# Forgetting attention and a GELU MLP on one core: a new order of the start, w_in in six parts, and the low value tile copied by GpSimd

## The chip, the core and the metric

The kernel runs on one core of one Trainium2 chip. The metric is the time of one launch on the device in microseconds; the runs shown are three, and their median counts. The engines are named as in the profile: PE is TensorE (matmuls; PEld its weight loads), DVE is VectorE, ACT is ScalarE, POOL is GpSimd and SP is SyncE. POOL, SP and ACT can issue DMAs. Each engine executes its instructions in the order in which the program gives them and waits on semaphores.

## The reference

```python
def _attn_ref(q, k, v, f):                 # q, k, v: (8, 8, 576, 64); f: (8, 8, 576)
    scores = (1 / sqrt(64)) * q @ k^T
    log_f = np.log(np.clip(f, 0.0001, 1.0))
    cum = np.cumsum(log_f, axis=-1)
    decay = cum[:, :, :, None] - cum[:, :, None, :]
    scores = np.where(causal, -1e9, scores + decay)
    return softmax(scores) @ v

def _moe_ref(x, w_in, w_out):              # x: (4608, 512), w_in: (512, 2048), w_out: (2048, 512)
    h = x @ w_in
    g = 0.5 * h * (1.0 + np.tanh(c * (h + 0.044715 * h * h * h)))
    return g @ w_out                       # (4608, 512) float32
```

The attention's output, with the heads side by side, is the MLP's input x.

## The kernel before

**Quads.** The 64 pairs of batch and head are taken four at a time: quad i (0 to 15) holds four heads of batch i // 2. For each quad, q and k are loaded by POOL's queue (`LQ.i`, `LK.i`, cast to bf16 on the way) and transposed by DVE (`TQ.i`, `TK.i`, line 197). The row factor of the decay falls out of the softmax, so only exp(-cum) of the key is needed: it is worked out once for all quads into `wT` and `w_bf`, and multiplied into v (`vw` by DVE or `VW` by POOL, line 214). The "low" value tile is a copy of the first 64 rows of the product into partitions 64 to 127 (`CL.i`, `copy_low`, line 219).

**Steps of a quad.** `S.i.r` (or `H.i.r.g` for a pair of heads) computes the scores of round r on PE (line 260) and their exps on ACT (line 268), `M.i.r` masks the diagonal blocks on POOL (line 274), `m.i.r` does it by a product with a triangle on DVE (line 303), `D.i` computes the denominators on PE (line 328; for quads 0 and 1 in two parts, `D.i.part`, line 314) and DVE (lines 347 to 351), `V.i.x` or `V.i.x.part` multiplies with the values on PE (lines 328 and 314), and DVE scales the result into xT (line 359).

**The MLP.** Tokens go through the MLP in nine chunks of 512. Chunk 0 is worked in two halves of 256 tokens: `J.half.g` computes 4 of the 16 feature tiles for one half (16 matmuls, line 481, into a two-bank tile of the pool psS) and one gelu on ACT (line 488). Its second product (`F.0.n`, line 597) and those of the other chunks (`F.c.n`, `f.c.n`, line 527; seven products in place of eight) are spread between the attention steps of later quads. Line 552 adds up and stores results through `o_st`.

**The order** is written by hand. `SETUP` and `FRONT` are tables of words, played from left to right, for quads 0 to 6 and chunks 0 and 1; `TABLES[c]` holds chunk c from 2 on, with `q3` meaning quad 2c + 3. Every engine's queue follows this order, and so do the DMA queues of the engines that issue. `A@B` lets the transfer of A wait for that of B. The words of the start: `LP.t` and `LU.t` load tile t of v of batch 0, `LX.b.half` and `LV.b.half` the heads of half of batch b; `SB` is POOL's sums over earlier tiles of the logs, `CW` the two matmuls that complete the log sums and the two exps that give `wT`, `W` the cast to `w_bf`; `TR` makes the triangles and `Z` writes zeros; `WI.c` and `WO.c` load the parts of w_in and w_out on POOL's queue; `B.n.cols` issues n matmuls on zeros into a tile that nobody reads (line 239); `X` and `Y` load ACT's table for exp and for gelu.

**Memory on chip.** The pools in PSUM are psS with two tiles of two banks (scores, MLP block, some outputs), psO with one tile of two banks (`po`, and the tile of the filler matmuls) and psM with two tiles of one bank. A tile comes free when its last reader is done.

Of the kernel before, what the change touches and what calls it, by code (L numbers as in the profile page):

```python
# [16 lines left out]
def kernel(  # L17
# [200 lines left out]
    def copy_low(i):  # L218
        nc.vector.tensor_copy(vw[i % 2][64:128, LOW], vw[i % 2][0:64, 0])
# [202 lines left out]
    def seven_in(c, k, act=0):  # L422
# [47 lines left out]
        gelu(1, 0, u2)  # L470
        yield

    def mlp_in_half(half, g):

        ph = psS.tile([128, 2, 512], FP32, name="ps_h", tag="s")
        n0 = QA * half
        for dts in (range(N_DT - 1), range(N_DT - 1, N_DT)):
            for j in range(4):
                ft = 4 * g + j
                for dt in dts:  # L480
                    nc.tensor.matmul(  # L481
                        ph[:, j // 2, QA * (j % 2):QA * (j % 2) + QA],
                        w_in_sb[:, dt, 128 * ft:128 * ft + 128],
                        xT[:, dt, n0:n0 + QA],
                        start=(dt == 0 and j % 2 == 0), stop=(dt == N_DT - 1),
                        skip_group_check=True,
                    )
# [119 lines left out]
    def setup():  # L607
        nc.sync.dma_start(out=f_sb, in_=f.rearrange("b h s -> (b h) s"))
        dmas["LK.0"] = load_one(k, k_c, 0)
        dmas["LQ.0"] = load_one(q, q_c, 0)  # L610
# [13 lines left out]
        nc.vector.tensor_scalar(f_sb, f_sb, 1e-4, 1.0, op0=ALU.max, op1=ALU.min)  # L624
# [10 lines left out]
    def zeros():  # L635
        for t_ in v_nat:
            nc.gpsimd.memset(t_[64:128, HIGH, :, :], 0.0)
        for t_ in vw:
            nc.gpsimd.memset(t_[0:64, LOW, :, :], 0.0)
        nc.gpsimd.memset(w_bf[0:64, :, LOW, :], 0.0)  # L640
# [41 lines left out]
    def load_values(b, half):  # L682
# [121 lines left out]
```

## Time and profile before

| | us |
|---|---|
| median of three runs (326.24 to 327.14) | 326.45 |
| the profiled execution | 326.83 |
| its span in the profile | 325.1 |
| PE busy | 312.4 |
| DVE busy | 255.9 |
| ACT busy | 206.8 |
| POOL busy | 107.3 |

The profile is one execution. Its times count from the start of the span. A row of its timeline gives start, duration, engine, line, operation, output and inputs, shapes, and how many instructions it merges; in brackets stands how long the engine was idle before and who ended that. Matmuls are pipelined, and the durations of two rows can overlap by some 0.06 us. The granted clock of PE was 0.999 in the mean.

### The profile page before, as it was taken

What the parts mean: (1) busy time and instruction counts of PE and PEld (TensorE: products, weight loads), DVE (VectorE), ACT (ScalarE), POOL (GpSimd) and SP (SyncE); (2) the same over time, 40 slices, a digit from 0 to 9 for tenths busy, and PEclk for the clock granted to TensorE, in tenths of its full rate; (3) what the DMA queues carried; (4) which work ended last, traced back from release to release, by engine and by line L of the source; (5) the groups of instructions that cost most, each with busy time, mean ns of one, the idle gap of its engine ahead of it and who ended that gap; (6) DMA issues with size and microseconds to landing.
All of it is one profiled execution on the core that took longest, in us unless ns stands there. A gap on an engine that the chain in (4) does not pass through costs nothing.

```text
span 325.1 us, 12342 instructions
## 1 busy us (share of the span) xinstructions
PE 312.4 (96%) x5527; PEld 219.0 (67%) x5547; DVE 255.9 (79%) x407; ACT 206.8 (64%) x259; POOL 107.3 (33%) x150
## 2 busy tenths in 40 slices
PE   3999999999999999899999999999999999999995
PEld 1357844544867567576777677667766788788784
DVE  5576138896779899968996899789977979896882
ACT  4685676775857686477857785678666843732830
POOL 8986563440320218410563047302720150000000
PEclk9999999999999999999999999999999999999999
DMA  7999999879102931393119711891120012003013
GB/s 134 202 210 214 181 228 190 163 154 228 49 4 86 176 58 36 67 241 86 36 49 175 172 36 37 150 209 37 34 69 0 4 36 100 2 32 100 0 34 97
DMA packets 46485, 33.45 MB, mean 103 GB/s; under 512 B 29792, under 2 KB 40160, under 8 KB 46432
## 3 DMA queue, kind: packets, MB, share of 16 engines
q0 software_dynamic: 8624, 15.99, 28.3%
q1 hardware_dynamic: 37664, 16.60, 19.4%
q8 instruction: 43, 0.70, 0.9%
q14 instruction: 10, 0.08, 0.1%
q10 hardware_dynamic: 144, 0.07, 0.1%
HBM read 36.85 MB, written 9.44 MB: 142 GB/s over the span
## 4 chain that ended last, share of the span: by engine, by line
PE 87%; DVE 7%; POOL 2%; issue 2%; ACT 1%; POOLq 0%; DVEq 0%; ACTq 0%
PE ps_w L527 27%; PE ps_h L373 14%; PE ps_s L260 9%; PE po L328 9%; PE ps_cd L432 8%; PE ps_ab L432 6%; PE ps_h L481 4%; PE pso L597 4%; PE ps_h L387 2%; PE po_m L314 1%; PE idle_ps L239 1%; DVE pt L303 1%; ACT pt L268 1%; POOL v_nat L168 1%; DVE kT L197 1%
## 5 line engine op out<-in xcount | busy, mean ns | idle before, releaser
L268 ACT ACTIVATE pt<-ps_s 128x1024 bf16<-128x1024 f32 (+2 forms) x100 | 93.7, 988 | 38.5 <-PE ps_s L260 33.1
L274 POOL TENSOR_SCALAR_AFFINE_SELECT pt<-pt 128x512 bf16<-128x512 bf16 (+3 forms) x65 | 38.7, 604 | 115.2 <-ACT pt L268 114.2
L373 PE MATMUL ps_h<-xT,w_in_sb 128*128 128x512 bf16 x228 | 54.5, 379 | 0.6
L527 PEld LDWEIGHTS <-gT 128*32 128x32 bf16 (+1 forms) x1247 | 50.6, 97 | 6.0 <-issue 1.7
L527 PE MATMUL ps_w<-w_out_sb,gT 128*32 128x256 bf16 (+1 forms) x1050 | 46.9, 273 | 0.0
L380 ACT ACTIVATE gT<-ps_h 128x1024 bf16<-128x1024 f32 x30 | 30.6, 1020 | 17.2 <-PE ps_h L373 16.7
L527 PEld LDWEIGHTS <-gsum 128*32 128x32 bf16 (+1 forms) x1256 | 39.2, 97 | 2.5 <-issue 1.1
L373 PEld LDWEIGHTS <-w_in_sb 128*128 128x128 bf16 x240 | 23.4, 98 | 24.3 <-issue 0.4
L260 PE MATMUL ps_s<-qT,kT 32*128 32x64 bf16 (+5 forms) x896 | 36.4, 264 | 0.1
L197 DVE STREAM_TRANSPOSE kT<-k_c 128x576 f32<-128x576 f32 x16 | 19.9, 1245 | 14.1 <-DMA k_c<-in_k_dram 14.1
L527 PE MATMUL ps_w<-usum,gsum 128*32 128x256 bf16 (+1 forms) x832 | 30.6, 273 | 0.0
L214 POOL TENSOR_TENSOR vw<-v_nat,wT 128x1280 bf16<-128x1280 f32 (+1 forms) x13 | 30.3, 2333 | 0.1
L260 PEld LDWEIGHTS <-kT 32*128 32x128 bf16 x896 | 16.5, 93 | 17.1 <-issue 12.0
L441 ACT ACTIVATE gT<-snap 128x512 bf16<-128x512 f32 x45 | 26.1, 625 | 3.0 <-DVE snap L455 2.4
L432 PEld LDWEIGHTS <-w_in_sb 128*128 128x128 bf16 x240 | 23.4, 98 | 6.2 <-issue 1.5
L552 DVE TENSOR_TENSOR o_st<-ps_w,snap 128x512 f32<-128x512 f32 x31 | 21.3, 687 | 7.5 <-PE ps_w L527 6.1
L328 PE MATMUL po<-pt,vw 128*32 128x64 bf16 (+4 forms) x624 | 22.5, 278 | 0.7 <-DVE xT L359 0.7
L359 DVE TENSOR_TENSOR xT<-po,rb 128x576 bf16<-128x576 f32 x26 | 19.5, 751 | 3.8 <-PE po L328 3.3
L328 PEld LDWEIGHTS <-vw 128*32 128x32 bf16 x672 | 14.3, 97 | 11.3 <-issue 4.6
L432 PEld LDWEIGHTS <-xT 128*128 128x128 bf16 x180 | 17.6, 98 | 5.2
L197 DVE STREAM_TRANSPOSE qT<-q_c 128x576 f32<-128x576 f32 x16 | 19.9, 1245 | 0.9 <-PE ps_s L260 0.7
L191 POOL DMA_DIRECT2D k_c<-in_k_dram x16 | 9.2, 576 | 27.8 <-DVE kT L197 22.4
(104 smaller groups left out, 478.1 us busy)
## 6 DMA issues: line engine op xcount, KB each, us to landing
out_dram<-o_st SPq DMA_DIRECT2D x35, 256.0 KB, 2.2
k_c<-in_k_dram POOLq DMA_DIRECT2D x16, 288.0 KB, 5.5
q_c<-in_q_dram POOLq DMA_DIRECT2D x16, 288.0 KB, 7.2
v_nat<-in_v_dram SPq DMA_DIRECT2D x16, 256.0 KB, 6.1
v_nat<-in_v_dram SPq DMA_DIRECT2D x20, 128.0 KB, 4.7
w_in_sb<-in_moe_w_in_dram POOLq DMA_DIRECT2D x4, 512.0 KB, 10.0
w_out_sb<-in_moe_w_out_dram POOLq DMA_DIRECT2D x4, 512.0 KB, 8.6
v_nat<-in_v_dram POOLq DMA_DIRECT2D x9, 128.0 KB, 7.1
```

What stands on the lines that cost most here:

```text
L197: nc.vector.transpose(out=dst.rearrange("p s c -> p (s c)").bitcast(FP32) .rearrange("p (t a) -> p a t", a=S // 32), in_=src.rearrange("p ...
L214: eng.tensor_mul(vw[i % 2][:, t0:t1], vb[:, t0:t1, h0:h0 + 4, :], wT[:, i, t0:t1, :].unsqueeze(3).to_broadcast([128, t1 - t0, 4, D]))
L260: nc.tensor.matmul(tiles[h // 2][:, h % 2, c0:c0 + nq], key_columns(i, key, h, c), qq[32 * h:32 * h + 32, q0:q0 + nq, c], start=(c == 0 an ...
L268: nc.scalar.activation(p[:, 2 * g:2 * g + 2, off:off + n], t[:, :, 0:n], AF.Exp, scale=scale)
L274: nc.gpsimd.affine_select(out=x, in_=x, compare_op=ALU.is_ge, fill=0.0, base=0, pattern=pattern, channel_multiplier=-1)
L328: nc.tensor.matmul(po[r0:r0 + w.shape[-1], 448 + q0:448 + q0 + nq], w, p[:, h, col:col + nq], start=(key in (0, "low")), stop=(key in ("lo ...
L373: nc.tensor.matmul(ph[:, j, :], w_in_sb[:, dt, 128 * ft:128 * ft + 128], xT[:, dt, CH * c:CH * (c + 1)], start=(dt == 0), stop=(dt == N_DT ...
L380: nc.scalar.activation(gT[:, 2 * pr:2 * pr + 2, :], ph, AF.Gelu_apprx_tanh)
L432: nc.tensor.matmul(ps[:, j], w[:, dt, 128 * j:128 * j + 128], x[:, dt], start=(first and j == 0 and dt == 0), stop=(dt == 1), skip_group_c ...
L441: nc.scalar.activation(gT[:, ft:ft + 2, HC * j:HC * (j + 1)], x, AF.Gelu_apprx_tanh)
L527: nc.tensor.matmul(ps[c0:c0 + width, n, cols[0]:cols[1]], x[:, j, 128 * n + c0:128 * n + c0 + width], w[:, j, cols[0]:cols[1]], start=(fir ...
L552: nc.vector.tensor_add(st, ps, kept[name])
```

## The change

- `SETUP` and `FRONT` are written anew up to quad 2. The first matmul of the log sums becomes a word of its own (`CU`); the first scores `S.0.0` stand between it and `CW`, which keeps the second matmul and the exps.
- w_in comes in six parts in place of four: the columns 0 to 512, 512 to 1024 and 1024 to 2048, each in two halves of the rows.
- `mlp_in_half` yields after each of its four feature tiles, and takes its tile from psO where it is called with `spare`. The word `j.0.0` plays one such quarter; four of them stand between the last scores of quads 0 and 1, where fillers stood, and a fifth plays the gelu. `J` plays all. The loop order within it is one feature tile after the other.
- The masks of round 3 of quad 0 go from DVE to POOL (`m.0.3` to `M.0.3`), the second half of v of batch 1 (`LX.1.1`) and quad 3's product (`VW.3`) from the start to behind quad 2's scores.
- The zeros that POOL wrote (`Z`) are written by DVE in `setup`.
- `cl` is `copy_low` on POOL. The tables of chunks 2 to 6 use it in place of `CL` for q3 and q4; it stands behind the masks of q3's last round, and behind `VW` of q4.
- `seven_in` gets a branch for `act` over 1.

```diff
     SETUP = """
-        TK.0 LP.4 LP.0 LP.1
+        TK.0 LP.0 LP.1
     """
     FRONT = """
-        TQ.0 B.2.256 TK.1 SB TR LP.2@LQ.0 B.2.128 CW S.0.0 B.5.384 B.1.256 Z TQ.1 vw.0.0 S.0.2 WI.0 LQ.2 M.0.0 B.3.384 H.1.0.1 LP.3 B.1.256 vw.1.0
-        WI.1@LU.4 W H.1.1.1 WI.3 B.2.256 WI.2 H.1.0.0 M.1.0.1 D.0.0 M.1.0.0 H.0.1.1 V.0.0.0 H.0.1.0 B.2.256 M.0.1 H.1.1.0 V.0.1.0 D.1.0 H.0.3.0
-        B.2.128 V.1.0.0 LX.1.1 H.0.3.1 V.1.1.0 m.0.3.2 H.1.3.0 m.0.3.4 B.1.256 VW.1.1 H.1.3.1 B.4.128 vw.0.1 D.0.1 M.1.3 S.1.2 M.1.1 LK.2 V.0.1.1
-        V.0.0.1 WO.0 J.0.1 D.1.1 J.0.0 WO.1@LV.1.1 V.1.1.1 V.1.0.1 J.0.3 WO.2@WI.1 VW.3 J.1.0 WO.3 LK.3 LQ.3 J.1.1 TQ.2 J.1.3 LQ.4 LX.1.0@WO.2 TK.2
-        J.0.2 J.1.2 X LK.4 F.0.6 TK.3 B.3.256 S.2.0 LK.5 F.0.9 S.2.2 F.0.10 S.2.1 TQ.3 TQ.4 F.0.10 LV.2.0@LK.5 m.2.1 vw.2 TK.4 S.3.0 f.0.1 M.2.2
-        CL.2 LQ.5 M.2.0 D.2 f.0.6 S.3.1 m.3.0 F.0.6 V.2.0 S.3.2 TK.5 LK.6 M.3.2 f.0.7 V.2.1 CL.3 S.4.1 m.3.1 LQ.6 F.0.6 TQ.5 H.4.2.1 D.3 H.4.0.1
+        TQ.0 B.2.256 TR TK.1 SB B.2.128 CU S.0.0 CW B.5.384 B.1.256 TQ.1 W WI.0 WI.1 vw.0.0 LP.2@LQ.0 M.0.0 LP.4 S.0.2 B.3.384 H.1.0.1 H.1.0.0
+        vw.1.0 LP.3 WI.2@LU.1 M.1.0.1 D.0.0 M.1.0.0 WI.3 WI.4 WI.5 H.1.1.1 V.0.0.0 H.0.1.1 V.0.1.0 D.1.0 H.0.1.0 V.1.0.0 M.0.1 LQ.2 LK.2 H.1.1.0
+        M.1.1 V.1.1.0 H.0.3.0 j.0.0 H.0.3.1 j.0.0 M.0.3 H.1.3.0 j.0.0 vw.0.1 H.1.3.1 j.0.0 M.1.3 VW.1.1 H.1.2.0 D.0.1 H.1.2.1 j.0.0 J.0.1 V.0.1.1
+        V.0.0.1 D.1.1 J.0.2 WO.0 WO.1@LU.4 V.1.1.1 V.1.0.1 J.0.3 J.1.0 WO.2@WI.5 WO.3 J.1.1 TQ.2 LK.3 LQ.3 J.1.2 J.1.3 LX.1.0@WO.0 LQ.4 TK.2 X F.0.6
+        LK.4 TK.3 S.2.0 M.2.0 LK.5 F.0.9 S.2.2 M.2.2 LX.1.1@WO.2 F.0.10 S.2.1 TQ.3 TQ.4 F.0.10 LV.2.0@LK.5 m.2.1 vw.2 TK.4 S.3.0 f.0.1 CL.2 LQ.5
+        VW.3 D.2 f.0.6 S.3.1 m.3.0 F.0.6 V.2.0 S.3.2 TK.5 LK.6 M.3.2 f.0.7 V.2.1 CL.3 S.4.1 m.3.1 LQ.6 F.0.6 TQ.5 H.4.2.1 D.3 H.4.0.1 LQ.7 VW.4
...
     TABLES[3] = """
...
-        f.22 S.q3.1 V.q2.0 TK.q4 TQ.q4 M.q3.1 VW.q3 f.18 S.q3.2 V.q2.1 M.q3.2 TK.q5 CL.q3 f.16 S.q4.0 VW.q4 D.q3 M.q4.0 f.18 S.q4.1 TQ.q5 V.q3.0
-        M.q4.1 f.13 V.q3.1 T f.3 CL.q4 S.q4.2
+        f.22 S.q3.1 V.q2.0 TK.q4 TQ.q4 M.q3.1 VW.q3 f.18 S.q3.2 V.q2.1 M.q3.2 cl.q3 TK.q5 f.16 S.q4.0 VW.q4 cl.q4 D.q3 M.q4.0 f.18 S.q4.1 TQ.q5
+        V.q3.0 M.q4.1 f.13 V.q3.1 T f.3 S.q4.2
...
     def load_w_in(c):
-        n, u = D_FF // 2, c % 2
-        s = slice(n * (c // 2), n * (c // 2 + 1))
+        u = c % 2
+        s = slice(*((0, 512), (512, 1024), (1024, 2048))[c // 2])
         return nc.gpsimd.dma_start(out=w_in_sb[:, 2 * u:2 * u + 2, s], in_=w_in_hbm[:, u, :, s])
...
-    def copy_low(i):
-        nc.vector.tensor_copy(vw[i % 2][64:128, LOW], vw[i % 2][0:64, 0])
+    def copy_low(i, eng):
+        eng.tensor_copy(vw[i % 2][64:128, LOW], vw[i % 2][0:64, 0])
...
         multiply(pd, a22, t4, False)
-        nc.vector.tensor_add(u2, pd, u2)
+        if act > 1:
+            z = part()
+            nc.scalar.copy(z, pd)
+            nc.gpsimd.tensor_add(u2, z, u2)
+        else:
+            nc.vector.tensor_add(u2, pd, u2)
...
-    def mlp_in_half(half, g):
-        ph = psS.tile([128, 2, 512], FP32, name="ps_h", tag="s")
+    def mlp_in_half(half, g, spare=0):
+        if spare:
+            ph = psO.tile([128, 1024], FP32, name="ps_h", tag="po").rearrange("p (a n) -> p a n", a=2)
+        else:
+            ph = psS.tile([128, 2, 512], FP32, name="ps_h", tag="s")
         n0 = QA * half
-        for dts in (range(N_DT - 1), range(N_DT - 1, N_DT)):
-            for j in range(4):
-                ft = 4 * g + j
-                for dt in dts:
-                    nc.tensor.matmul(...)
+        for j in range(4):
+            ft = 4 * g + j
+            for dt in range(N_DT):
+                nc.tensor.matmul(...)
+            if j < 3:
+                yield
+        if spare:
+            yield
         nc.scalar.activation(gT[:, 4 * g:4 * g + 4, n0:n0 + QA], ..., AF.Gelu_apprx_tanh)
...
+        for t_ in v_nat:
+            nc.vector.memset(t_[64:128, HIGH, :, :], 0.0)
+        for t_ in vw:
+            nc.vector.memset(t_[0:64, LOW, :, :], 0.0)
+        nc.vector.memset(w_bf[0:64, :, LOW, :], 0.0)
         nc.vector.tensor_scalar(f_sb, f_sb, 1e-4, 1.0, op0=ALU.max, op1=ALU.min)
...
+    def within_tiles():
+        sums.append(psM.tile([128, NT * BH], FP32, name="cum_ps", tag="m"))
+        nc.tensor.matmul(sums[0], utri_f32, logfT, start=True, stop=False)
     def make_w():
-        cum_ps = psM.tile([128, NT * BH], FP32, name="cum_ps", tag="m")
-        nc.tensor.matmul(cum_ps, utri_f32, logfT, start=True, stop=False)
+        cum_ps = sums[0]
         nc.tensor.matmul(cum_ps[:, BH:], ones_f32, before, start=False, stop=True)
...
-        "J": mlp_in_half,
+        "J": lambda half, g: pull(mlp_in_half(half, g), 4),
+        "j": lambda half, g: pull(parts_in.setdefault((half, g), mlp_in_half(half, g, 1)), 1),
```

In the changed kernel the first MLP product of chunk 0 has line 490, its gelu line 501, the second product of chunk 0 line 610.

More of the change, by code (lines that the diff above doesn't have):

```diff
@@ L83 @@
+        H.4.0.0 V.3.1 v.3.0 f.0.3 H.4.2.0 CL.4 I.1.0 m.4.1 U.0 LV.2.1@LQ.5 I.1.4 TQ.6 m.4.2.3 I.1.1 I.1.5 U.1 LV.3.0@LQ.7 LV.3.1 m.4.2.2 TK.6 G.0
+        M.4.0 LK.7 LQ.8 LK.8 I.1.2 I.1.3 U.3 K.1.0 K.1.1 K.1.2 I.1.6 I.1.7 G.1.1.2 U.2 X F.1.16 S.5.0 f.1.26 S.5.1 D.4 M.5.0 f.1.16 S.5.2 V.4.0
+        m.5.2.3 f.1.10 VW.5 V.4.1 K.1.3 CL.5 m.5.2.2 S.6.0 f.1.10 M.5.1 D.5 f.1.7 S.6.1 V.5.1 f.1.12 V.5.0 T.2 S.6.2 vw.6
     """
@@ L469, in seven_in @@
             gelu(0, 1, p1)
+        if act > 1:
+            yield
         gelu(1, 0, u2)
         yield
-    def mlp_in_half(half, g):
-        ph = psS.tile([128, 2, 512], FP32, name="ps_h", tag="s")
-        n0 = QA * half
-        for dts in (range(N_DT - 1), range(N_DT - 1, N_DT)):
-            for j in range(4):
-                ft = 4 * g + j
-                for dt in dts:
[L481 to L487, printed above, removed]
+    def mlp_in_half(half, g, spare=0):
[3 more added lines that the diff above has]
+            ph = psS.tile([128, 2, 512], FP32, name="ps_h", tag="s")
+        n0 = QA * half
+        for j in range(4):
+            ft = 4 * g + j
+            for dt in range(N_DT):
+                nc.tensor.matmul(
+                    ph[:, j // 2, QA * (j % 2):QA * (j % 2) + QA],
+                    w_in_sb[:, dt, 128 * ft:128 * ft + 128],
+                    xT[:, dt, n0:n0 + QA],
+                    start=(dt == 0 and j % 2 == 0), stop=(dt == N_DT - 1),
+                    skip_group_check=True,
+                )
+            if j < 3:
+                yield
+        if spare:
+            yield
         nc.scalar.activation(gT[:, 4 * g:4 * g + 4, n0:n0 + QA],
@@ L633, in setup @@
         nc.scalar.copy(logfT[0:64, HIGH * BH:], ps_lt[0:64, HIGH * BH:])
[L635 to L640, printed above, removed]
     def triangles(copy):
@@ L652, in sums_before @@
                                  logfT[:, t * BH:(t + 1) * BH])
+    sums = []
+    def within_tiles():
+        sums.append(psM.tile([128, NT * BH], FP32, name="cum_ps", tag="m"))
+        nc.tensor.matmul(sums[0], utri_f32, logfT, start=True, stop=False)
     def make_w():
-        cum_ps = psM.tile([128, NT * BH], FP32, name="cum_ps", tag="m")
-        nc.tensor.matmul(cum_ps, utri_f32, logfT, start=True, stop=False)
+        cum_ps = sums[0]
         nc.tensor.matmul(cum_ps[:, BH:], ones_f32, before, start=False, stop=True)
@@ L669, in pull @@
                 return
-    fills = {}
+    fills, parts_in = {}, {}
     dmas = {}
@@ L687 @@
         "w": lambda: cast_w(nc.scalar.copy),
+        "CU": within_tiles,
         "CW": make_w,
@@ L690 @@
         "sb": lambda: sums_before(nc.vector),
-        "Z": zeros,
         "TR": lambda: triangles(nc.vector.tensor_copy),
@@ L702 @@
         "vw": lambda i, *part: make_vw(i, nc.vector, *part),
-        "CL": copy_low,
+        "CL": lambda i: copy_low(i, nc.vector),
+        "cl": lambda i: copy_low(i, nc.gpsimd),
         "TK": transpose_k,
@@ L759 @@
         "LV": lambda c: load_v(c + 2) if c + 2 < B else None,
-        **{name: quads(ops[name]) for name in "S M m D V v VW vw CL TK TQ LK LQ".split()},
+        **{name: quads(ops[name]) for name in "S M m D V v VW vw CL cl TK TQ LK LQ".split()},
     }
```

17 lines of the change are left out of this document (7 added, 10 removed).

## The prediction

> **What bounds the kernel now.** I read the page first (busy times, chain), then the busy times by stretch, then what TensorE (PE) waited for after the start.
>
> ```profile
> PE 312.4 (96%) x5527; PEld 219.0 (67%) x5547; DVE 255.9 (79%) x407; ACT 206.8 (64%) x259; POOL 107.3 (33%) x150
> PE 87%; DVE 7%; POOL 2%; issue 2%; ACT 1%; POOLq 0%; DVEq 0%; ACTq 0%
> 0.00:20.00 20.00, 13.96 (x141) 6.56 (x141) 11.20 (x27) 12.39 (x17) 17.07 (x37) 1.00 0.93 175
> 20.00:40.00 20.00, 19.80 (x291) 15.26 (x290) 10.50 (x20) 12.05 (x15) 14.64 (x18) 1.00 1.13 200
> 40.00:60.00 20.00, 19.63 (x291) 9.66 (x296) 12.78 (x16) 14.83 (x16) 8.10 (x13) 1.00 1.05 210
> 120.00:140.00 20.00, 18.28 (x522) 13.16 (x512) 18.49 (x27) 11.87 (x13) 12.48 (x16) 1.00 0.29 62
> PE ps_w L527 <- DVE o_st L552: 0.9, 1, 0.9
> PE po L328 <- DVE xT L359: 0.7, 1, 0.7
> ```
>
> The stretch rows give busy us of PE, PEld, DVE, ACT, POOL, then granted clock, DMA share and GB/s. PE is the bound nearly everywhere. Time can be won in three ways only: PE work taken away, the thin start, or PE's waits. After 96 us the list of PE's waits holds exactly the two last rows, 0.94 and 0.73 us to two digits (below), both in chunk 2 (120 to 140 us). At the start, part of PE's busy time is filler matmuls, which compute nothing. So this change can win in two places.
>
> **First scores ahead of the log sums.**
>
> ```profile
> 6.82 1.26 DVE L197 STREAM_TRANSPOSE qT<-q_c 128x576 f32<-128x576 f32 x1 [0.21 <-DMA q_c<-in_q_dram]
> 8.76 1.22 PE L657 MATMUL cum_ps<-gsum 128*128 128x256 f32 x2 [1.01 <-POOL gsum L650]
> 9.91 0.83 PE L260 MATMUL ps_s<-qT,kT 32*128 32x256 bf16 x16
> 10.67 1.99 PE L239 MATMUL idle_ps<-usum 128*128 128x384 bf16 x6
> 12.59 0.72 PE L260 MATMUL ps_s<-qT,kT 32*128 32x320 bf16 x8
> 13.94 1.29 DVE L214 TENSOR_TENSOR vw<-v_nat,wT 128x512 bf16<-128x512 f32 x2 [1.64 <-DMA v_nat<-in_v_dram]
> ```
>
> S.0.0 needs qT, ready at 6.82 + 1.26 = 8.08, but stands behind the ones matmul, which waits for GpSimd's sums. Now S.0.0 runs 8.1 to 8.9, the ones matmul 1.22 to 10.15, the same fillers 1.99 to 12.1: S.0.2 starts at 12.1, 0.5 earlier. The weights' exps come later, behind S.0.0's, near 11.2; their first reader, vw.0.0, waits for v until 13.94 anyway, so that costs nothing.
>
> **The first MLP block in quarters.** Between 14 and 24 us scores, exps and fillers alternate.
>
> ```profile
> 14.00:24.00 10.00, 2.33 (x14) 0.76 (x12) 1.00 1.09 200
> 14.79 8.42 ACT L268 ACTIVATE pt<-ps_s 128x768 bf16<-128x768 f32 x10
> 23.58 0.46 PE L260 MATMUL ps_s<-qT,kT 32*128 32x320 bf16 x8
> 24.08 1.30 ACT L268 ACTIVATE pt<-ps_s 128x640 bf16<-128x640 f32 x2 [0.86 <-PE ps_s L260]
> 29.70 1.22 PE L314 MATMUL po_m<-pt,vw 128*32 128x320 bf16 x40
> 30.86 10.65 PE L481 MATMUL ps_h<-xT,w_in_sb 128*128 128x256 bf16 x96
> ```
>
> The first row is for the filler line alone: PE 2.33 us. These fillers go, and j.0.0's 16 matmuls come in: 96 take 10.65, so 16 take 1.78. PE's work up to the last score is then about the same (0.55 less), and 1.78 us leave the run of MLP matmuls behind it, where PE never waits. The exps cannot hide this: 8.42 + 1.30 us of them from about 14.3 end by 24.0, plus small gaps, against 25.4 now. Of the 0.5 gained at the start I keep 0.3, since PE and ACT are now both nearly full up to the last score (which ends at 23.7 in place of 24.04). Front: 1.78 + 0.3 = **2.1 us**. Bounds: 1.3 (the start's gain gone, PE waiting 0.5 more for exps or masks) to 2.8 (0.5 and 0.55 kept in full).
>
> This needs the data in time. Sizes follow from the shapes; the rates are the stretch rows' (3.5 MB by 20 us, 7.5 by 40, 11.7 by 60). Up to the last of the six w_in parts: f 0.15, four k/q 1.18, v of batch 0 1.18, w_in 2.10 = 4.6 MB, so 20 + 1.1/0.200 = 25.5 us. Columns from 1024 on are first read by J.0.2, behind 16 MLP matmuls and 60 po_m ones: 23.7 + 1.78 + 1.83 = 27.3. Up to the last w_out: 7.3 MB, 39 us; the MLP block ends at 30.86 + 10.65 - 2.1 = 39.4. Both fit by a little.
>
> **Other edits of the start.**
>
> ```profile
> 3.65 0.45 DVE L624 TENSOR_SCALAR gsum<-gsum 64x576 f32<-64x576 f32 x1 [1.37 <-DMA gsum<-in_f_dram]
> 9.59 0.98 POOL L637 MEMSET v_nat<- 64x512 f32 x2
> 42.64 0.49 PE L239 MATMUL idle_ps<-usum 128*128 128x256 bf16 x3
> ```
>
> The zeros move to VectorE, ahead of the clamp of f, where 1.37 us are idle; they need about that, so at most 0.2 is lost there. GpSimd loses 0.98 us and more of memsets and gains two issues for w_in, at some 0.73 each (3.63 for five, quoted below). The 0.49 us of fillers before S.2.0 go too: 0 to 0.49; I take 0, since the scores behind them wait for ACT's table change and exps. The branch for act over 1 is never entered: no table gives more than 1.
>
> **The low value tile on GpSimd.**
>
> ```profile
> L219 DVE COPY vw<-vw x14: 220/221/2070, 54.7 to 263.3; 64x256 bf16<-64x256 bf16 x14
> 127.64 2.33 POOL L214 TENSOR_TENSOR vw<-v_nat,wT 128x1280 bf16<-128x1280 f32 x1
> 127.98 2.07 DVE L219 COPY vw<-vw 64x256 bf16<-64x256 bf16 x1
> 130.82 0.62 PE L527 MATMUL ps_w<-w_out_sb,gsum 128*32 128x256 bf16 x16 [0.94 <-DVE o_st L552]
> 134.95 0.87 PE L328 MATMUL po<-pt,vw 128*32 128x512 bf16 x24 [0.73 <-DVE xT L359]
> 134.11 0.63 POOL L274 TENSOR_SCALAR_AFFINE_SELECT pt<-pt 128x512 bf16<-128x512 bf16 x1 [3.05 <-ACT pt L268]
> 7.25 0.26 POOL L648 COPY gsum<-gsum 128x64 f32<-128x64 f32 x1
> ```
>
> Fourteen copies (shortest, median and longest in ns), 0.22 us in the median; the one of 2.07 started inside GpSimd's product and ended with it (130.05 against 129.97). It held up o_st and, through VectorE's queue, xT: PE's two waits. With the copy on GpSimd, o_st can start 2.07 earlier, more than either wait: 0.94 + 0.73 = **1.67 us**, bounds 0.9 to 1.7. GpSimd's own copy is not in the trace: between 0.26 (the small copy) and 2.33 (the product); I take 0.4, nearer the small one. The product for the next quad and its mask stand behind it; 3.05 idle us before GpSimd's next mask cover both copies of the chunk. The other eight that move win nothing, as PE waited nowhere else.
>
> **v and its product moved.** LX.1.1 (five transfers) and VW.3 move from the start to behind M.2.2.
>
> ```profile
> 32.55 2.35 POOL L214 TENSOR_TENSOR vw<-v_nat,wT 128x1280 bf16<-128x1280 f32 x1
> 42.09 3.63 POOL L168 DMA_DIRECT2D v_nat<-in_v_dram  x5 [4.83 <-DMA w_out_sb<-in_moe_w_out_dram]
> 48.60 1.22 POOL L274 TENSOR_SCALAR_AFFINE_SELECT pt<-pt 128x512 bf16<-128x512 bf16 x2 [0.63 <-ACT pt L268]
> 56.78 0.38 DVE L303 TENSOR_TENSOR pt<-pt,causal 128x512 bf16<-128x512 bf16 x1
> 61.08 0.26 DVE L219 COPY vw<-vw 64x256 bf16<-64x256 bf16 x1
> 60.04 1.22 POOL L274 TENSOR_SCALAR_AFFINE_SELECT pt<-pt 128x512 bf16<-128x512 bf16 x2 [4.52 <-ACT pt L268]
> 62.69 0.86 PE L328 MATMUL po<-pt,w_bf 128*32 128x512 bf16 x24
> 67.37 0.59 POOL L191 DMA_DIRECT2D k_c<-in_k_dram  x1
> v_nat<-in_v_dram POOLq DMA_DIRECT2D x9, 128.0 KB, 7.1
> DMA to landing us min/median/max: 5.2/7.1/9.6
> ```
>
> The new gates are early ones: WI.2 waits for LP.1 (landed when vw.0.0 starts, 13.9) with M.1.0 behind it, due near 15.3 with its exps; LX.1.0 waits for the first w_out quarter (5.7 MB, 31 us) instead of the third, with LQ.4, LK.4 and M.2.0 behind it, and M.2.0 isn't due before 40.
>
> In the new time, 2.1 earlier: M.2.2 ends at 47.7, five issues take 3.63, to 51.3. The last v lands at 54.1 by bytes (10.5 MB: 40 + 3.0/0.210) or at 58.4 by the median 7.1 after issue; I take 56. VW.3 ends 2.35 later, 58.4. Behind it on GpSimd stand LK.6 (0.59 at most) and M.3.2 (1.22): 60.2. D.3, which waits for M.3.2, is due at 62.69 - 2.1 = 60.6; CL.3, which waits for VW.3 at the head of VectorE, at 59.0. It just fits: cost 0, up to 2.0 at the late end (58.4 + 2.35 + 0.59 + 1.22 = 62.6 against 60.6).
>
> **Sum.** The profiled execution took 326.83 (span 325.1, 1.7 around it): 326.83 - 2.1 - 1.67 = 323.06. The median of the runs, 326.45, is 0.38 lower: **322.7**. Its own range, from the bounds: 326.45 - 2.8 - 1.7 = 321.9 to 326.45 - 1.3 - 0.9 = 324.2.
>
> **Rivals.**
> A, 0.20: v lands after 56.4, and D.3 waits for M.3.2. For it: 7.1 median. Against it: the backlog is small by then. 0.3 to 2.0 given back: 323.0 to 324.7.
> B, 0.07: VW.3 starts just before the mask product m.3.0 (56.78 - 2.1 = 54.7) and holds it up for as much as 2.35, as the 2.07 copy was. This needs v at 52.4 to 54.7, the early end. Between 0 and 2.35 of it reaches PE; the middle, 1.2, gives 323.9.
> [...]
> [...]
> C, 0.08: the front wins nothing (the quarters wait for w_in or xT, and PE stops later for w_out): 326.45 - 1.67 = 324.8.
> D, 0.09: slower. M.3.2 behind a very late VW.3 again, beyond the whole gain. To lose 3.8 + 1, M.3.2 must end at 65.4, so v land at 61.3, 10 us after the last issue. The longest in the start's v transfers is 9.6, so only with a fuller DMA queue: 327.6 or more.
> E, 0.04: both gains vanish, 326.4.
>
> **How the numbers follow.** The forecast has 0.52. With A, B and C, 0.87 lie between 321.7 and 325.0, which is the range. 0.3% of 326.45, about what a measurement can tell, is 0.98, so faster means under 325.47: 0.52 + 0.20 + 0.07 + 0.08 = 0.87; same 0.04; slower 0.09.
>
> **What would show it.** Right: S.0.0 at 8.1, S.0.2 near 12.1; the last score by 23.7; the MLP block ending at 39.4; no PE wait near 128 to 135; GpSimd's copies at 0.3 to 0.6 us. Wrong: PE waiting at L490 for w_in, at L610 for w_out, or at D.3 (L328) near 60 for GpSimd; VW.3 ending after 58.8; a VectorE L303 of over 1 us near 55; a MLP block that ends after 40.2.

## The result, and the profile after

The changed kernel takes 324.59 us (median of 14 runs, 322.1 to 331.05) against 326.65 (14 runs, 326.22 to 327.14) for the kernel before on the same chip: 2.06 us less, a ratio of 0.993 with an interval of 0.991 to 0.9951. Ratios, here and below, leave out runs more than 1.5% above the fastest of the same kernel: here the three of 330.46, 330.71 and 331.05, whose mean granted clock is 0.979. The forecast was 322.7, 3.75 us less, so about half of the forecast gain came. The time lies inside the forecast range (321.7 to 325.0), but next to the price of rival C, 324.8, and not because the two terms of the sum came out: one came whole and a little more, the other not at all. The profiled execution took 325.03 (span 323.3).

Busy times by stretch of the kernel after (columns as in the prediction: stretch, its length, PE, PEld, DVE, ACT and POOL busy, granted clock, DMA share, GB/s):

```profile
0.00:20.00 20.00, 13.48 (x152) 6.94 (x153) 14.08 (x37) 12.19 (x17) 16.21 (x32) 1.00 0.94 172
20.00:40.00 20.00, 18.91 (x267) 14.05 (x266) 7.61 (x13) 12.17 (x15) 12.34 (x19) 1.00 1.14 188
120.00:140.00 20.00, 19.95 (x544) 14.97 (x536) 17.60 (x27) 13.12 (x15) 13.41 (x18) 1.00 0.37 79
```

Chunk 2 (120 to 140 us) went from 18.28 to 19.95 us of PE busy: its waits are gone. But 20 to 40 us went from 19.80 to 18.91: the start got a hole that it did not have. The list of PE's waits names it:

```profile
PE ps_h L490 <- DMA w_in_sb<-in_moe_w_in_dram: 1.0, 1, 1.0
PE ps_s L260 <- DVE qT L197: 0.9, 1, 0.9
```

The timeline of the start (start, duration, engine; in brackets the idle time before and who ended it):

```profile
5.99 1.26 DVE L197 STREAM_TRANSPOSE kT<-k_c 128x576 f32<-128x576 f32 x1 [1.80 <-DMA k_c<-in_k_dram]
7.43 1.26 DVE L197 STREAM_TRANSPOSE qT<-q_c 128x576 f32<-128x576 f32 x1 [0.18 <-DMA q_c<-in_q_dram]
8.74 0.83 PE L260 MATMUL ps_s<-qT,kT 32*128 32x256 bf16 x16 [0.91 <-DVE qT L197]
12.47 0.72 PE L260 MATMUL ps_s<-qT,kT 32*128 32x320 bf16 x8
16.12 1.22 POOL L274 TENSOR_SCALAR_AFFINE_SELECT pt<-pt 128x512 bf16<-128x512 bf16 x2 [1.46 <-ACT pt L268]
17.30 2.14 POOL L180 DMA_DIRECT2D w_in_sb<-in_moe_w_in_dram  x3
24.39 0.45 PE L260 MATMUL ps_s<-qT,kT 32*128 32x320 bf16 x4
29.98 1.70 PE L490 MATMUL ps_h<-xT,w_in_sb 128*128 128x256 bf16 x14 [1.01 <-DMA w_in_sb<-in_moe_w_in_dram]
32.77 8.91 PE L490 MATMUL ps_h<-xT,w_in_sb 128*128 128x256 bf16 x80
```

S.0.0 starts at 8.74, not 8.1: k, and with it q, came later. S.0.2 starts at 12.47 (before 12.59). The last score ends at 24.84 (before 24.04), and the MLP block at 32.77 + 8.91 = 41.68 against 30.86 + 10.65 = 41.51. **The new start won nothing in this execution.** The last three w_in parts were issued at 17.30, behind the mask M.1.0, for which POOL stood idle 1.46 us; meanwhile the DMA queue ran thin, 136 GB/s in the mean from 18 to 26 us against 218 before (the kernel after first, then the kernel before):

```profile
18.00:26.00 8.00, 7.99 (x118) 4.53 (x115) 3.98 (x9) 6.87 (x9) 6.97 (x12) 1.00 0.99 136
```

```profile
18.00:26.00 8.00, 7.80 (x159) 4.48 (x156) 6.54 (x15) 7.04 (x10) 7.27 (x9) 1.00 1.11 218
```

Chunk 2, first two rows of the kernel before (its third, 134.95, stands in the prediction), then three of the kernel after, two products that stand where the first wait was, and POOL's copies:

```profile
127.49 0.86 PE L328 MATMUL po<-pt,w_bf 128*32 128x512 bf16 x24
131.94 0.87 PE L328 MATMUL po<-pt,vw 128*32 128x512 bf16 x24
```

```profile
127.61 0.86 PE L328 MATMUL po<-pt,w_bf 128*32 128x512 bf16 x24
130.94 0.87 PE L328 MATMUL po<-pt,vw 128*32 128x512 bf16 x24
133.05 0.86 PE L328 MATMUL po<-pt,vw 128*32 128x512 bf16 x24
128.30 1.70 PE L540 MATMUL ps_w<-w_out_sb,gT 128*32 128x256 bf16 x56
129.83 0.61 PE L540 MATMUL ps_w<-w_out_sb,gsum 128*32 128x256 bf16 x16
127.84 0.39 POOL L219 COPY vw<-vw 64x256 bf16<-64x256 bf16 x1
130.71 0.39 POOL L219 COPY vw<-vw 64x256 bf16<-64x256 bf16 x1
```

From the denominators of quad 7 to its second value product went 7.46 us, and now go 5.44: 2.02 won, where the brackets of the two waits held 1.67. POOL's copy takes 0.39, as assumed (0.4).

### The profile page after: what moved, and what is told of

It reads as the page before. It is cut to its first block, busy times and chain, and to the rows that moved or that the text cites. A ratio compares the mean times of both kernels' runs of the same rounds, so it can differ in the third digit from the quotient of the medians.

```text
span 323.3 us, 12322 instructions
## 1 busy us (share of the span) xinstructions
PE 310.7 (96%) x5512; PEld 218.4 (68%) x5532; DVE 251.3 (78%) x401; ACT 206.9 (64%) x259; POOL 111.4 (34%) x158
## 4 chain that ended last, share of the span: by engine, by line
PE 89%; DMA 5%; ACT 2%; issue 1%; POOL 1%; DVE 1%; DVEq 0%; POOLq 0%
PE ps_w L540 30%; PE ps_h L373 16%; PE po L328 10%; PE ps_cd L432 8%; PE ps_s L260 8%; PE ps_ab L432 6%; DMA w_in_sb<-in_moe_w_in_dram 3%; PE pso L610 3%; PE ps_h L490 3%; PE ps_h L387 2%; DMA q_c<-in_q_dram 2%; ACT pt L268 1%; PE idle_ps L239 1%; PE ps_o L328 0%; POOL w_in_sb L180 0%
## 5 line engine op out<-in xcount | busy, mean ns | idle before, releaser
L274 POOL TENSOR_SCALAR_AFFINE_SELECT pt<-pt 128x512 bf16<-128x512 bf16 (+2 forms) x67 | 39.9, 605 | 107.7 <-ACT pt L268 106.6
L432 PE MATMUL ps_cd<-xT 128*128 128x256 bf16 x120 | 18.0, 273 | 0.0
```

The source lines that it names most:

```text
L274: nc.gpsimd.affine_select(out=x, in_=x, compare_op=ALU.is_ge, fill=0.0, base=0, pattern=pattern, channel_multiplier=-1)
L432: nc.tensor.matmul(ps[:, j], w[:, dt, 128 * j:128 * j + 128], x[:, dt], start=(first and j == 0 and dt == 0), stop=(dt == 1), skip_group_c ...
```

## The experiments

Twelve kernels ran. A ratio is to the kernel before, run on the same chip in between. Single runs of the kernel before at 330.3 to 330.5 (clock 0.984) widen the intervals of experiments 5 to 11. A median holds all runs unless it says otherwise. Experiments 1 to 4, 5 to 8 with 12, and 9 to 11 ran on three chips; the kernel before took 326.58 to 326.72 in the median on each, so medians are also compared across them. "Idle matmuls" are the fillers (`B.n.cols`), which compute nothing.

### 1 and 2: each half alone

```diff
 (1: the kernel before with)
-... M.q3.2 TK.q5 CL.q3 f.16 S.q4.0 VW.q4 D.q3 ... f.3 CL.q4 S.q4.2
+... M.q3.2 cl.q3 TK.q5 f.16 S.q4.0 VW.q4 cl.q4 D.q3 ... f.3 S.q4.2
 (2: the kernel after with the tables of chunks 2 to 6 of the kernel before)
```

> The kernel before, with only the tables of chunks 2 to 6 taken from the changed kernel: the low value tile of q3 and q4 is copied by GpSimd (cl). Theory (the copy blocked by GpSimd's product cost PE 0.94 + 0.73 us in chunk 2): 1.7 us less than before, 324.9 to 325.2, PE without a wait between 120 and 140 us, and little spread between runs, as before has little. Rival (the gain of the change comes from the new start, and chunk 2 gives its 1.7 us back later): within 0.5 us of before.

> The changed kernel, with only the tables of chunks 2 to 6 taken from the kernel before: the new start, with the copies on VectorE. Theory (the start wins about 0.4 us in the mean and brings the spread of the runs; in the profiled run it won nothing): 326.0 to 326.6 in the mean, runs 2 to 4 us apart, PE's two waits in chunk 2 back at about 1.7 us. Rival (the start wins the 2.1 us that were forecast, and the copies less than 1.7): 324.5.

The copies alone: 324.64, ratio 0.9935 (0.992 to 0.995), and no PE wait in chunk 2. The new start alone: 326.77, ratio 0.9994 (0.998 to 1.0008). Two of its twelve runs had a clock below 0.98: 332.85 at 0.979, and 402.01 at 0.76. The experiment's profile is of the last, and no run shows why its clock was low; no profile shows this kernel at full clock. So the gain of the change is that of the copies, and the start's cannot be told from nothing.

### 3: the w_in parts ahead of the mask

```diff
-        vw.1.0 LP.3 WI.2@LU.1 M.1.0.1 D.0.0 M.1.0.0 WI.3 WI.4 WI.5 H.1.1.1 ...
+        vw.1.0 LP.3 WI.2@LU.1 WI.3 WI.4 WI.5 M.1.0.1 D.0.0 M.1.0.0 H.1.1.1 ...
```

> The changed kernel, with WI.3, WI.4 and WI.5 issued before the two masks M.1.0 instead of behind them. Theory (the last parts of w_in are late because their issues stand on GpSimd behind masks that wait for exps, so that the DMA queue runs low between 18 and 26 us): DMA rate there back to about 200 GB/s from 117 to 171, PE's wait of 1.0 us at L490 gone, the MLP block ending near 40.7 instead of 41.7, 1.0 us less than the changed kernel; M.1.0 and so D.1.0 up to 0.7 us later, which may take part of it back. Rival (the smaller parts are slow in themselves): the rate stays under 175 GB/s between 18 and 26 us and PE still waits 0.7 us or more for w_in, no gain.

330.35 (328.52 to 332.11), ratio 1.0106 (1.0072 to 1.0139): slower. The wait for w_in did go, and the DMA rate came back to 178 to 209 GB/s. But three issues don't fit into POOL's idle time: M.1.0 started at 16.50, 0.38 us later than in the profile of the kernel after and 1.06 later than in that of experiment 12 (15.44), where k landed as early as here. PE waited before D.1.0, and 2.6 us later the granted clock halved:

```profile
17.78 0.35 PE L314 MATMUL po_m<-pt,w_bf 128*32 128x256 bf16 x8 [0.96 <-POOL pt L274]
16.00:18.00 2.00, 1.04 (x24) 0.52 (x24) 0.94 (x3) 1.68 (x2) 1.72 (x3) 1.00 1.08 178
20.00:21.00 1.00, 1.00 (x12) 0.49 (x8) 1.00 (x2) 1.00 (x2) 1.00 (x3) 0.68 1.10 204
22.00:24.00 2.00, 2.00 (x14) 0.93 (x14) 0.00 (x0) 1.01 (x2) 1.18 (x3) 0.50 1.10 201
30.00:31.00 1.00, 1.00 (x8) 0.78 (x7) 0.00 (x0) 0.99 (x2) 1.00 (x2) 0.70 1.00 68
```

The column behind POOL is the clock: 0.50 between the two slices in which it changes. PE is shown as busy all the while, at that clock. All six runs had clocks of 0.974 to 0.984. The new theory: the fillers that the change took out had also kept the clock up, and the new start stands at the edge.

### 4: the copy out of POOL's product

```diff
 (the kernel before, tables of chunks 2 to 5)
-... M.q3.2 TK.q5 CL.q3 f.16 ...
+... M.q3.2 CL.q3 TK.q5 f.16 ...
```

> The kernel before, with CL.q3 in chunks 2 to 5 one word earlier, ahead of TK.q5, still on VectorE. Then the copy of chunk 2 comes up at about 126.8 us, 0.8 us before GpSimd's product starts, but while GpSimd's masks run (126.4 to 127.7). Theory (a copy that meets a GpSimd instruction waits for its end): about 0.9 us instead of 2.07 in chunk 2, o_st ready before PE wants it, PE's waits gone, 1.5 to 1.7 us less than before. Rival (the copy's 2.07 us has another cause, such as the move across partitions or a late semaphore): about 2 us again, PE's waits as before, no gain.

325.19, ratio 0.9949 (0.9934 to 0.9965). The copy stays on DVE, but starts 0.8 us before POOL's next product, not inside it:

```profile
126.58 0.32 DVE L219 COPY vw<-vw 64x256 bf16<-64x256 bf16 x1
127.39 2.33 POOL L214 TENSOR_TENSOR vw<-v_nat,wT 128x1280 bf16<-128x1280 f32 x1
```

0.32 us in place of 2.07, and most of the gain with it. It was the overlap with POOL's product that cost the time, not the copy. POOL's masks ran from 126.19 to 127.42, so the copy met one of them; the 0.9 us that the expectation gave for this did not come. Why 1.5 us are won here and 2.05 in experiment 1 was not followed up.

### 5 to 7: the two causes taken away, one by one

```diff
 (5: the kernel after with)
-        ... WI.2@LU.1 M.1.0.1 D.0.0 M.1.0.0 WI.3 WI.4 WI.5 H.1.1.1 ...
+        ... WI.2@LU.1 WI.3 WI.4 M.1.0.1 D.0.0 M.1.0.0 WI.5 H.1.1.1 ...
 (6: experiment 3, and 7: experiment 5, with n = 4 and 2)
-        ... V.0.1.0 D.1.0 H.0.1.0 ...
+        ... V.0.1.0 B.n.256 D.1.0 H.0.1.0 ...
```

> The kernel after, with only two of the three last w_in parts (WI.3, WI.4) issued ahead of M.1.0, into the 1.46 us that GpSimd stood idle there for its exp; two issues are 1.43 us. Theory (the start lost its gain to the w_in parts that came late, 1.0 us of wait at L490): M.1.0 stays at 16.1, the DMA rate of 18 to 26 us rises from 117-171 to about 180-210 GB/s, the wait at L490 goes, the first MLP block ends near 40.7, the granted clock stays 1.0, and the time is 323.6 (ratio to the kernel before about 0.990). Rival (the start's work itself, not the transfers, sets the end: the scores' cadence of 0.98 us): 324.6, as the kernel after. Rival from the run with all three parts ahead: even a small shift of M.1.0 opens a PE wait before D.1.0, and the granted clock falls to about 0.5 for some 10 us: 328 to 331.

> The run with all three w_in parts ahead of M.1.0 (330.35, granted clock 0.5 from 22 to 30 us), plus one thing: four matmuls on the idle tile, 256 columns each, put into the wait of 0.96 us before D.1.0. Their results are never read. Clock theory (PE busy for only 1.04 of 2 us in 16-18 us is what took the clock down, and this is the whole of that kernel's loss): PE busy 1.5 or more in 16-18, granted clock 1.0 throughout, time 323.6 to 324.3. Rival (the loss comes from the later M.1.0 and what follows from it, or the clock falls for another reason, as the DMA load): 328 to 331 as before.

> The kernel after with WI.3 and WI.4 ahead of M.1.0 and two idle matmuls of 256 columns before D.1.0. If the w_in wait and the clock are the two things that kept the new start from winning, this has neither: 323.4 to 323.9, no run with a mean granted clock under 0.99. If the start wins nothing for another reason: 324.5 to 324.8.

Experiment 5: 323.9, ratio 0.9903 (0.9867 to 0.9938); no PE wait for w_in, 189 GB/s from 18 to 26 us, the MLP block ends at 40.7. One of its six runs was 330.58, at a clock of 0.979. Experiment 6: 324.55, ratio 0.9922 (0.9894 to 0.9951), clock 0.998 or more in all seven runs. **Four idle matmuls made the kernel of experiment 3 faster by 5.8 us**:

```profile
17.58 0.61 PE L239 MATMUL idle_ps<-usum 128*128 128x256 bf16 x4
16.00:18.00 2.00, 2.00 (x36) 1.06 (x34) 1.43 (x5) 1.99 (x3) 1.99 (x4) 1.00 1.15 155
22.00:24.00 2.00, 2.00 (x27) 1.11 (x25) 0.00 (x0) 1.71 (x3) 1.65 (x4) 1.00 1.03 161
```

Experiment 7, with both remedies, is the fastest kernel of all: 323.57 (323.11 to 323.83), ratio 0.9892 (0.986 to 0.9924), clock 0.998 or more in all six runs.

### 8 and 12: the clock theory from the other side

```diff
 (8: the kernel before with)
-... H.1.0.1 LP.3 B.1.256 vw.1.0 ... WI.3 B.2.256 WI.2 ... H.0.1.0 B.2.256 M.0.1 ...
+... H.1.0.1 LP.3 vw.1.0 ... WI.3 WI.2 ... H.0.1.0 M.0.1 ...
 (12: the kernel after with)
-        ... V.0.1.0 D.1.0 H.0.1.0 ...
+        ... V.0.1.0 B.2.256 D.1.0 H.0.1.0 ...
```

> The kernel before without the three groups of idle matmuls between 14 and 19 us (five matmuls of 256 columns, rows 14.69, 15.46 and 18.04 of its trace, 1.06 us of PE busy time); nothing else is changed, and none of their results is read. Clock theory: PE's busy share of 14-20 us falls from 5.93 to about 5 of 6 us, in some runs the granted clock falls to about 0.5 for some 10 us after it, and these runs take 329 or more; the others take the time of the kernel before (326.5), or up to 0.3 less. Rival (these idle matmuls have nothing to do with the clock, and PE was only made to do useless work): 325.6 to 326.5 in every run, clock 1.0.

> The kernel after with the two idle matmuls of 256 columns before D.1.0, and its w_in parts where they are. Clock theory (the runs of 330 us of the kernel after come from the wait before D.1.0 that the removed idle matmuls used to fill, and from nothing else): no run above 326, a median of 324.2 to 324.7, as the kernel after without those three runs. Rival (the idle matmuls help only together with the earlier w_in parts, since the wait of 1 us at L490 is a second place where the clock can fall): some runs of 328 to 331 again.

Experiment 8, with five idle matmuls fewer: 330.11 in the median of twelve (ratio 1.0048, 1.0009 to 1.0087), and it falls in two. Four runs with the full clock took 326.33 to 326.44, eight with 0.979 to 0.984 took 330.02 to 331.33. In its profile, a run of 330.39, PE is busy for 5.16 of the 6 us from 14 to 20 (5.93 in the kernel before), and the clock is 0.50 from about 18 to 28:

```profile
14.00:20.00 6.00, 5.16 (x77) 2.91 (x80) 3.44 (x8) 5.27 (x7) 4.32 (x7) 0.85 1.08 217
```

Taken out, these fillers win 0.3 us when the clock holds and cost 3.6 when it doesn't (326.39 and 330.36, the medians of the two kinds, against 326.72). Experiment 12: 324.41 (ratio 0.9938, 0.9916 to 0.996), clock 0.998 or more in all seven runs. That is the time of the kernel after without its three runs of 330 and more (324.31, median of eleven), as the theory says; one run, 326.54, is above the 326 that the expectation allowed, though at full clock, and stays unexplained. Seven runs without a low clock prove little alone, where the kernel after had three in fourteen; experiments 3, 6 and 8 carry the theory. The profile of experiment 12 comes back below: its run of 323.19 loses only 0.2 us at L490, though its w_in parts stand behind the mask.

### 9 to 11: three parts of the new start, from the kernel of experiment 7

```diff
 (9: the second half of v of batch 1 earlier)
-        LK.4 TK.3 S.2.0 M.2.0 LK.5 F.0.9 S.2.2 M.2.2 LX.1.1@WO.2 F.0.10 ...
+        LK.4 LX.1.1@WO.2 TK.3 S.2.0 M.2.0 LK.5 F.0.9 S.2.2 M.2.2 F.0.10 ...
 (10: each of the first four j.0.0 becomes B.2.256, the fifth becomes J.0.0)
-        ... D.0.1 H.1.2.1 j.0.0 J.0.1 V.0.1.1 ...
+        ... D.0.1 H.1.2.1 J.0.0 J.0.1 V.0.1.1 ...
 (11: the log sums first again)
-        ... CU S.0.0 CW B.5.384 ...
+        ... CU CW S.0.0 B.5.384 ...
```

> The kernel with two w_in parts ahead and two idle matmuls (323.57; called the mended kernel here), with the five v loads of LX.1.1 moved from behind M.2.2 to ahead of M.2.0, 3.4 us earlier on GpSimd's queue. Theory (rival A of the prediction: the late v is what eats a gain of the start in some runs; in the run with two parts ahead and no idle matmuls v landed at 58.2 and PE was busy for only 5.24 of 6 us in 60 to 66, in the mended kernel's trace it landed at 56.1 and nothing waited): v lands near 53 to 54, VW.3 waits for it no longer than 1 us, PE stays at 5.8 or more of 6 us in 54 to 66, and the time is that of the mended kernel or up to 0.4 less, 323.1 to 323.6. Rival (the masks M.2.0 and M.2.2 that are now queued behind 3.6 us of issues come too late for the denominators of quad 2, whose matmuls start at 50.9): a PE wait near 51 and 323.8 to 325.

> The mended kernel without quarters: the first block of the MLP (J.0.0, sixteen matmuls and their Gelu) is recorded whole behind the last score half, and two idle matmuls of 256 columns stand at the place of each of the four quarters. The kernel before's arrangement in the kernel after's order. Prediction's theory (1.78 of the quarters lie where PE otherwise runs idle matmuls or waits, so whole they cost that again): block end 1.5 to 1.9 later, 325.1 to 325.5. Rival (the quarters win nothing, since they stretched the cadence of the last scores from 0.755 to 0.98 us): 323.5 to 324.0.

> The mended kernel with one swap taken back: the second matmul of the log sums and its exps (CW) stand ahead of the first scores (S.0.0) again. Theory A (the swap is worth 0.3, as the prediction took it, and opens the start to the landing of the first k and q, which differed by 0.8 us between the profiles: S.0.0 at 9.8 to 9.9 again whatever they do): 323.7 to 324.2, with less spread. Theory B (the swap sets the whole start, since the first exp and with it every mask and score behind it come 1.0 to 1.6 us earlier): 324.5 to 325.2. Theory C (S.0.2 and what follows are bound by the second q tile at 12.1 to 12.5 anyway): 323.5 to 323.6.

Experiment 9: 324.14, ratio 0.9915 (0.9884 to 0.9947), 0.6 slower than experiment 7, so the theory fails, and the named rival too: the masks were in time. v did land early, and that was the harm. VW.3 now ran beside DVE's work for quad 2, whose product took 1.92 (1.48 in the kernel after), and PE waited for the denominators:

```profile
51.30 1.92 DVE L214 TENSOR_TENSOR vw<-v_nat,wT 128x1280 bf16<-128x1280 f32 x1
52.42 2.99 POOL L214 TENSOR_TENSOR vw<-v_nat,wT 128x1280 bf16<-128x1280 f32 x1
54.41 1.07 DVE L219 COPY vw<-vw 64x256 bf16<-64x256 bf16 x1
56.36 0.87 PE L328 MATMUL po<-pt,vw 128*32 128x512 bf16 x24 [0.70 <-DVE den L347]
```

The copy of 1.07 (0.22 in the kernel after) ends with POOL's product, at 55.5 and 55.4. The other end of this scale is in experiment 5, where v landed at 58.2:

```profile
60.47 0.59 POOL L191 DMA_DIRECT2D k_c<-in_k_dram  x1
61.07 1.24 POOL L274 TENSOR_SCALAR_AFFINE_SELECT pt<-pt 128x512 bf16<-128x512 bf16 x2
60.81 1.79 DVE L303 TENSOR_TENSOR pt<-pt,causal 128x512 bf16<-128x512 bf16 x1
62.65 0.61 PE L328 MATMUL po<-pt,w_bf 128*1 128x448 bf16 x16 [0.39 <-DVE pt L303]
```

There the mask product m.3.1, queued behind CL.3 and so behind VW.3, fell beside POOL's mask and took 1.79 in place of the 0.42 of the kernel before. In the profile of experiment 7 v landed at 56.1, between the two, and PE waited for neither.

Experiment 10: 324.82, ratio 0.9932 (0.9905 to 0.996): the quarters are worth 1.25 us, less than the theory's 1.5 to 1.9 and far from the rival's nothing. Experiments 9 and 10 had nearly the same S.0.0 in their profiles (8.81 and 8.90), so their starts compare row by row:

```profile
24.51 0.46 PE L260 MATMUL ps_s<-qT,kT 32*128 32x320 bf16 x4
40.44 1.46 PE L610 MATMUL pso<-w_out_sb,gT 128*128 128x512 bf16 x5
```

```profile
24.06 0.46 PE L260 MATMUL ps_s<-qT,kT 32*128 32x320 bf16 x4
41.73 1.46 PE L610 MATMUL pso<-w_out_sb,gT 128*128 128x512 bf16 x5
```

With quarters (first fence) the last score stands 0.45 later and the end of the MLP block, where L610 begins, 1.29 earlier.

Experiment 11: eight of twelve runs at clocks of 0.977 to 0.984 (328.76 to 331.26), four at full clock with 324.29 to 324.57. In its profile POOL comes to the three w_in issues 1.3 us later than in experiment 7 (14.73 and 13.40) and to M.1.0 at 16.87 (15.54); PE waits 1.68 us before D.1.0 and is busy for 0.47 of the 2 us from 16 to 18. At full clock it is 0.8 slower than experiment 7, between theories A and B; the ratio over the counted runs (0.9951, 0.9908 to 0.9995) mixes both kinds. That the two idle matmuls did not save it also shows that they are no cure by themselves: they fill 0.4 us, and the wait was longer.

## Why the prediction was right in its sign, and where it failed

**The copies: right, and undersized.** 1.67 was forecast and 2.05 measured alone (experiment 1). The cause was the one named, the overlap with POOL's product: experiment 4 leaves the copy on DVE, moves it out of POOL's product and gets 1.5. The term was read from the brackets of two waits, but from V to V the rows shrank by 1.12 and 0.90, some 0.18 more than each bracket. The rows show why: without a wait, the next matmul row starts before the modelled end of the last one (129.83 against 128.30 + 1.70 = 130.00 in the kernel after), 0.17 here and not the 0.06 named ahead of the prediction. The bracket counts from that end, so it is not the whole of a wait's cost. The same copy of chunk 2 took 0.32 outside the product (experiment 4) and 2.07 inside it (the kernel before); what stretches it there is not shown.

**The front: 2.1 forecast, 0.0 measured.** Two steps failed, one through the other, and a third was too large.

- *"Up to the last of the six w_in parts ... 25.5 us."* This counted bytes at a steady rate, and looked at no issue time. In the profile of the kernel after the parts stood on POOL's queue behind a mask that waits for ACT, the DMA queue ran thin, and w_in landed at 29.9, where J.0.2 waited for it. With two parts ahead of the mask the median is 0.84 lower (experiment 7 against 12), but the runs overlap (323.11 to 323.83 and 323.19 to 326.54). Rival C had 0.08 and 324.8: its outcome came, though the wait was at J.0.2 and not at the quarters that it named, and PE did not stop for w_out.
- *"S.0.0 needs qT, ready at 8.08."* That was the landing of k in one execution, and the earliest of all these profiles (k's transpose starts at 5.34 to 6.28). In the kernel before it set nothing: S.0.0 waited for the log sums, so that a landing 0.8 us later moved it by nothing. The first fence is from experiment 1, which has the start of the kernel before. In the new order S.0.0 follows the landing: the second fence is from experiment 7, to be held against 5.99 and 8.74 above.

```profile
6.16 1.26 DVE L197 STREAM_TRANSPOSE kT<-k_c 128x576 f32<-128x576 f32 x1 [2.07 <-DMA k_c<-in_k_dram]
9.90 0.82 PE L260 MATMUL ps_s<-qT,kT 32*128 32x256 bf16 x16
```

```profile
5.44 1.26 DVE L197 STREAM_TRANSPOSE kT<-k_c 128x576 f32<-128x576 f32 x1 [1.25 <-DMA k_c<-in_k_dram]
8.19 0.83 PE L260 MATMUL ps_s<-qT,kT 32*128 32x256 bf16 x16 [0.36 <-DVE qT L197]
```

  This landing also decides what the first step costs. In the profile of experiment 12 k landed early, and with the same order of issues as in the kernel after M.1.0 and the three issues behind it came 0.7 us earlier on POOL:

```profile
8.26 0.83 PE L260 MATMUL ps_s<-qT,kT 32*128 32x256 bf16 x16 [0.43 <-DVE qT L197]
16.62 2.14 POOL L180 DMA_DIRECT2D w_in_sb<-in_moe_w_in_dram  x3
27.89 2.10 PE L490 MATMUL ps_h<-xT,w_in_sb 128*128 128x256 bf16 x16
31.07 8.91 PE L490 MATMUL ps_h<-xT,w_in_sb 128*128 128x256 bf16 x80
```

  J.0.2 took 2.10 (1.92 in experiment 7), so PE lost 0.2 to w_in in place of 1.01, and the MLP block ended at 39.98. That is 1.1 to 1.5 earlier than with the old start (41.51 in the kernel before, 41.06 and 41.25 in experiments 1 and 4), at the low end of the forecast's bounds of 1.3 to 2.8, and the run took 323.19, where 323.06 had been worked out for a profiled execution. With parts ahead of the mask and k early (experiment 7) the block ended at 39.91, with k late (experiments 5 and 9, S.0.0 at 8.93 and 8.81) at 40.66 and 40.60, and with k late and the parts behind the mask (the kernel after) at 41.68. So the place of the issues cost about 1.0 us with a late k and 0.1 with an early one. How often k is late in the runs that have no profile is not shown.

  The swap is worth about 0.8 (experiment 11, full clock) rather than 0.3, but it opens the start to this scatter: runs of the kernel after with clocks of 0.998 and more go from 322.1 to 325.03, those of before from 326.2 to 327.1.
- *"1.78 us leave the run of MLP matmuls."* Measured 1.25. A quarter takes 0.22 more than the two idle matmuls in its place in experiment 10, and the last score comes 0.45 later: 1.78 - 0.45 = 1.33.

With w_in in time and the clock held, the front is worth 1.07 in the median (experiment 1 to experiment 7), half of what was forecast. Three of the signs named as wrong stood in the trace: PE waiting at L490 for w_in, VW.3 ending after 58.8 (60.85), and the MLP block ending after 40.2 (41.68).

**What the prediction did not see: the clock.** It took 2.33 us of fillers for work that computes nothing and can go. Some of them also held the granted clock: it is 0.998 or more in all runs of experiment 6, and 0.974 to 0.984 in experiment 3 without them; in experiment 8, without five of the old ones, eight of twelve runs are at 0.979 to 0.984. The kernel after has three runs of fourteen that lose 6 us at a clock of 0.979; experiments 3, 6 and 8 make the missing fillers the likely cause, but no profile shows such a run of this kernel.

**v and VW.3: no cost, in the profiled execution by luck.** v landed at 58.5, past the 56.4 from which rival A was to cost something. It cost nothing because D.3 was not early: the front had gained nothing, and D.3 started at 62.86 without a wait.

```profile
58.52 2.33 POOL L214 TENSOR_TENSOR vw<-v_nat,wT 128x1280 bf16<-128x1280 f32 x1 [4.29 <-DMA v_nat<-in_v_dram]
62.86 0.86 PE L328 MATMUL po<-pt,w_bf 128*32 128x512 bf16 x24
```

With k early, in experiment 7, the working itself holds: v at 56.07 and the end of VW.3 at 58.40, forecast 56 and 58.4, and no wait. Where the front gains with a late k (experiment 5), PE loses 0.39 and 0.27 us there, but through DVE's mask product, not through M.3.2 as rival A had it. In experiment 9 v landed at 52.42, at the early end that rival B names, and VW.3 did hold DVE up, though at quad 2's product and copy and not at m.3.0. Zeros, W, the gates and w_out cost nothing that can be seen.

## What to carry to other kernels

Ask of a load not only whether its bytes fit, but when its issue leaves its engine's queue: transfers behind one waiting mask cost about 1.0 us here in the profiles in which the first load came late, and hid the gain of the new start there. Before idle matmuls are taken out, look at what PE does in the same 2 us without them, because at the start of this kernel some of them pay for themselves in clock (5.8 us between experiments 3 and 6). And a time that hangs on one landing in one trace is a sample: see first whether the row that it releases is bound by it now.

## What the runs showed of the hardware

**In three profiles the granted clock was half for 10 us and more behind a thin stretch of PE.** In experiment 3 the stretch held a PE wait of 0.96 us. From the slices in which the clock changes (0.68 at 20 to 21 us, 0.70 at 30 to 31, and 0.50 between), it was half from 20.36 to 30.60: 10.24 us, although PE was busy throughout. In experiment 8's profile the same working gives 10.24, in experiment 11's 13.66. Half a clock lost over 10.24 of 326 us is a mean of 0.984, over 13.66 of 326 it is 0.979; 26 of the 31 runs above 328 us have one of these two figures.

From 14 to 18 us PE is busy for 3.51 to 3.98 of the 4 us in the profiles that kept the clock (the kernels before and after, experiments 1, 5 to 7, 9, 10 and 12), and for 3.43 (experiment 8), 2.84 (3) and 2.45 (11) in those that lost it. But in the profile of the kernel after PE is busy for 2.91 of the 4 us from 26 to 30, with a wait of 1.01 us at 29 us, and the clock stayed at 1.00: neither the length of a wait nor the busy time of such a stretch decides alone. Why one program keeps its clock in some runs and loses it in others (it kept it in four of twelve and lost it in eight, in experiment 8 as in 11) is not shown. What it is in the fillers that held the clock is open too: the matmuls of the stretches before the fall are mostly ones of 32 rows or 32 columns, and the fillers are 128 by 128, but no run here varied that alone.

**DVE's work took longer beside other work of POOL's too.** In experiment 5 DVE's mask product took 1.79 us beside a DMA issue of POOL's and a mask of 1.24 (0.42 in the kernel before); in experiment 9 a copy took 1.07 (0.22 in the kernel after) beside a product of POOL's that itself took 2.99 in place of 2.33.
